# Turning eleven row blocks of a weight gradient by DMA transposes instead of TensorE transposes

## The chip, the core and the metric

One core of one Trainium2 chip runs one program: the forward pass and all gradients of a small stack of layers. The metric is the device time of one execution in microseconds. A kernel is run several times; the median is given with the lowest and highest. A profile is one execution recorded by the hardware; its span is the time from the first to the last instruction.

The engines have short names in the profile's rows: PE is TensorE (PEld its weight loads), DVE is VectorE, ACT is ScalarE, POOL is GpSimd and SP is SyncE, which here does nothing but issue DMA transfers. Each engine works through its own list of instructions in order. A "q" behind the name (SPq) marks the engine's queue of waits and DMA issues.

## The reference

Two layers are applied twice each: A, a gated long convolution (an SSM of H3 kind), and B, a dense layer with SiLU. Each has a layer norm ahead of it and a residual around it. The program returns the output and the gradients of eight inputs.

```python
def _B_ref(x, w1, w2):
    h = jnp.einsum("bsd,df->bsf", x, w1)
    h = _silu(h)
    out = jnp.einsum("bsf,fd->bsd", h, w2)
    return out

x = A_q
x = x + _A_ref(_layernorm(x, axis=-1), A_k, A_v, A_shift_k, A_ssm_k, A_ssm_D)
x = x + _B_ref(_layernorm(x, axis=-1), B_w1, B_w2)
x = x + _A_ref(_layernorm(x, axis=-1), A_k, A_v, A_shift_k, A_ssm_k, A_ssm_D)
x = x + _B_ref(_layernorm(x, axis=-1), B_w1, B_w2)
...
_out, _vjp = jax.vjp(_f, A_q, A_k, A_v, A_shift_k, A_ssm_k, A_ssm_D, B_w1, B_w2)
_grads = _vjp(grad_out)
```

The sizes are S = 2048 rows, D = 448 channels and F = 1792 hidden units, all in bf16. The gradient of `w1` has D rows and F columns. It is the sum over both uses of layer B of norm(x) transposed times the gradient of `h`.

## The kernel before

The program has three stages. `_ssm_prefix` (to about 100 us) makes the spectra of the convolution by products with Fourier matrices. `Main.run` then goes through four chunks of 512 rows, forward and backward. Last comes `_ssm_suffix` (from about 500 us), which takes the gradient of the convolution back through the spectra and makes the gradients of k, v, the shift weights, the convolution kernel and the skip weights.

The gradients of the two weights of layer B don't hang on that last stage. They are cut into small pieces by the class `Jobs`, and `jobs.run(n)` sprinkles n pieces between the suffix's own TensorE work. The order of TensorE's instructions is the order in which the program is written (`manual_schedule`). For the other engines the Tile framework's scheduler orders instructions when the program is built; on the chip each engine follows that fixed order.

One piece is four products with 128x128 stationary blocks (`mms`, L1038). The gradient of `w1` is made transposed: for each of 14 row blocks `ft` of 128 hidden units, a PSUM bank `ps_d` of 128 x 448 gathers 16 products of the stationary operand `g_d1` with the normalized rows `n3m`, then 16 of `g_d0` with `n1m` (the two uses of layer B). Each set of 16 stationary blocks is one load of 512 KB from DRAM into one of four `dstat` buffers (`load`, L1030), issued by SP as soon as TensorE is through with the load four before.

When a row block is done, `fin_w1` copies the bank to SBUF on ScalarE (`dout`, L1112, three buffers in turn) and calls `flush` for the row block before it, which thus is turned one block late. `flush` turns 128 hidden units x 448 channels into 448 channels x 128 hidden units: four TensorE transposes (L1125) of 112 columns each into the PSUM bank `ps_dt`, a ScalarE copy into one of four SBUF buffers `do7` (shown as `wts`, since they lie in that tile, L1127) and a store to the output issued by POOL (L1128). `do7` has 112 partitions, one for each of the 112 channels of a quarter.

POOL's queue also carries other stores of the suffix, among them `gkv` (L1268) and `gk` (L1254), whose SBUF buffers are reused two or four units later. ACT's queue carries the load of `kx_s` (L1275 and L1277) and the stores of `gK` (L1295). A DMA transpose is already used elsewhere: `_turn_grad` (L131, L132) turns rows of 448 channels straight from DRAM in two transfers, the first of three 128-channel blocks, the second of the last 128 channels (320 to 448, so that 64 channels come twice); `store` (L595) turns larger SBUF tiles.

Of the kernel before, what the change touches and what calls it, by code (L numbers as in the profile page):

```python
# [17 lines left out]
P = 128  # L18
# [5 lines left out]
DC = 112  # L24
ND = 4
# [88 lines left out]
def _copy(nc, eng, out, in_):  # L114
    if eng is nc.scalar:
        return nc.scalar.copy(out, in_)  # L116
    return eng.tensor_copy(out, in_)  # L117
# [18 lines left out]
def kernel(  # L136
# [63 lines left out]
    with tc.manual_schedule(engines={nc.tensor.engine}):  # L200
        with ExitStack() as es:
            Main(k, es).run(ys)
        _ssm_suffix(k)
# [790 lines left out]
class Jobs:  # L994
# [121 lines left out]
    def flush(self):  # L1116
        nc, k = self.nc, self.k
        if self.pend is None:
            return
        ft, o = self.pend  # L1120
        self.pend = None
        out7v = k.outs[7].rearrange("(c p) f -> p c f", p=DC)
        pt = k.psum.tile([DC, ND, P], BF16, name="ps_dt", tag="tr", bufs=2)
        for dc in range(ND):
            nc.tensor.transpose(pt[:, dc, :], o[:, dc * DC:(dc + 1) * DC], k.ident[:])  # L1125
        o7 = k.do7[ft % 4]
        _copy(nc, nc.vector if ft == 13 else nc.scalar, o7, pt[:])  # L1127
        (nc.scalar if ft == 13 else nc.sync if ft == 12 else nc.gpsimd).dma_start(out=out7v[:, :, ft * P:(ft + 1) * P], in_=o7)  # L1128


def _s1_gy(k, rows):
# [6 lines left out]
def _ssm_suffix(k):  # L1138
    nc, tc, bal = k.nc, k.tc, k.bal
# [7 lines left out]
    with ExitStack() as es:  # L1147
# [4 lines left out]
        gks = sp.tile([P, 19, D], BF16, name="gks")  # L1152
        ws = k.wtp.tile([P, 6144], BF16, name="wts", tag="WT")
        kk1 = ws[:, 0:4096].rearrange("p (a b) -> p a b", a=2)
        k.do7 = [ws[:DC, 4096 + 512 * i:4608 + 512 * i].rearrange("p (a b) -> p a b", a=ND) for i in range(4)]
        B1k = A1[:].rearrange("p a c n s -> p (a c n s)").rearrange("p (q d) -> p q d", d=D)
        for _ in _s1_gy(k, range(12, 16)):
            jobs.run(2)
# [18 lines left out]
        for g in range(7):  # L1177
            pt = psum.tile([P, 2, 16, 64], BF16, name="ps_tr", **mm)
# [188 lines left out]
```

## Time and profile before

| what | value |
|---|---|
| time, median of 3 runs | 704.69 us (704.58 to 705.24) |
| the profiled run's own time | 704.52 us |
| its span | 702.7 us, 14555 instructions, granted TensorE clock 0.997 |
| TensorE products ps_d, L1038, in all | 896, 353 ns listed each |
| TensorE transposes ps_dt, L1125 | 56 (14 row blocks x 4), 216 to 264 ns listed each |
| ScalarE copy of ps_dt, L116 | 13, 585 to 614 ns each |
| VectorE copy of ps_dt, L117 (row block 13) | 1, 424 ns |
| stores of w1's gradient, L1128 | 14 of 112 KB: 12 by POOL (707 to 747 ns to issue each), 1 by SP, 1 by ACT |
| loads of dstat for w1's gradient | 28 of 512 KB, median 5.4 us from issue to landing |
| queue q1 (hardware, SP's transfers) | 184550 packets, 111.78 MB, 58.3% of 16 engines' span |

The listed time of one matmul is from its start to its modelled end, and neighbours overlap in TensorE's pipeline; what one costs a full stream is the distance from its start to the next start. An instruction on a queue of SP, ACT or POOL that issues a transfer is listed with the time that issuing it took; the transfer lands later, and the rows of DMA issues give that time. A row of waits names the waiting instruction, what released it, the total in microseconds, how many times, and the longest. Times in a timeline are microseconds from the span's start. The row blocks of w1's gradient run from 580 to 695 us of the span.

### The profile page before, as it was taken

The numbers are of one execution on the slowest core, as the hardware profiler recorded it, in microseconds if no ns is written. First come the engines' busy times: TensorE is split into PE (matmuls) and PEld (weight loads), VectorE is DVE, ScalarE is ACT, GpSimd is POOL, SyncE is SP. The second block draws the span as 40 slices with busy tenths as digits, with TensorE's granted clock in tenths as the row PEclk, the third lists the DMA queues.
The fourth block names the chain that finished last, engine by engine and source line by source line (L and its number), as shares of the span: only waits on it lengthen the run. The fifth ranks groups of instructions, "written<-read, shape, count | busy, mean of one in ns | idle before, by whom it ended". The sixth has DMA issues, their size and how long they took to land.

```text
span 702.7 us, 14555 instructions
## 1 busy us (share of the span) xinstructions
PE 671.8 (96%) x5897; PEld 359.8 (51%) x5933; DVE 484.3 (69%) x1131; ACT 432.2 (62%) x522; POOL 101.0 (14%) x173
## 2 busy tenths in 40 slices
PE   6998789999999999999999999999999999999996
PEld 5876555454444444444444334444555555555664
DVE  5689862676889948889568884753946555538991
ACT  4988766968866957669577585223655453554431
POOL 1047110110011100111100100010111211102311
PEclk9999999999999999999999999999999999999999
DMA  8999948459898987487676599959567888966981
GB/s 315 260 272 304 351 137 212 112 109 260 217 225 240 245 195 184 137 236 202 203 180 180 159 227 335 288 168 218 187 225 268 309 273 317 349 190 215 330 292 42
DMA packets 199797, 161.03 MB, mean 229 GB/s; under 512 B 147697, under 2 KB 180212, under 8 KB 198962
## 3 DMA queue, kind: packets, MB, share of 16 engines
q1 hardware_dynamic: 184550, 111.78, 58.3%
q0 software_dynamic: 10368, 36.29, 15.2%
q10 hardware_dynamic: 4812, 12.04, 5.2%
q8 instruction: 46, 0.75, 0.4%
q14 instruction: 21, 0.17, 0.1%
HBM read 66.05 MB, written 54.60 MB: 172 GB/s over the span
## 4 chain that ended last, share of the span: by engine, by line
PE 59%; DVE 19%; issue 10%; ACT 5%; DMA 3%; POOL 3%; ACTq 0%; POOLq 0%; DVEq 0%
PE ps_d L1038 18%; PE ps_n L828 9%; PE ps_h L638 7%; PE ps_g L638 6%; PE ps_o L790 5%; DMA w2sb<-in_B_w_dram 3%; DVE ln_st L301 2%; PE ps_v L265 2%; PE ps_cv L449 2%; POOL rstd L306 2%; DVE lb_v L986 2%; PE ps_h L642 2%; DVE n L309 1%; DVE X L794 1%; PE ps_g L642 1%
## 5 line engine op out<-in xcount | busy, mean ns | idle before, releaser
L1038 PEld LDWEIGHTS <-dstat 128*128 128x128 bf16 x896 | 84.0, 98 | 77.8 <-issue 4.0
L828 PE MATMUL ps_n<-w1T,ghT 128*128 128x448 bf16 x448 | 97.0, 353 | 1.6 <-DVE ghT L813 1.3
L790 PE MATMUL ps_o<-w2sb,aT 128*128 128x448 bf16 x448 | 89.3, 353 | 0.2
L638 PE MATMUL ps_h<-nT,w1sb 128*128 128x512 bf16 (+1 forms) x408 | 84.2, 336 | 3.5 <-ACT Dall L116 2.2
L116 ACT CAST ghT<-ps_g 128x1024 bf16<-128x1024 f32 (+1 forms) x54 | 47.8, 900 | 59.4 <-PE ps_g L642 40.2
L638 PE MATMUL ps_g<-nT,w2T 128*128 128x512 bf16 x319 | 78.0, 380 | 2.1 <-DVE Dall L117 0.5
L828 PEld LDWEIGHTS <-ghT 128*128 128x128 bf16 x448 | 40.7, 98 | 50.5 <-issue 8.0
L790 PEld LDWEIGHTS <-aT 128*128 128x128 bf16 x448 | 43.0, 98 | 40.7 <-issue 2.6
L638 PEld LDWEIGHTS <-w1sb 128*128 128x128 bf16 x420 | 39.2, 98 | 39.0 <-issue 9.8
L773 ACT ACTIVATE aT<-ps_h 128x1024 bf16<-128x1024 f32 (+1 forms) x48 | 44.2, 920 | 20.4 <-PE ps_h L642 12.7
L986 DVE SCALAR_TENSOR_TENSOR lb_v<-lb_u,n 128x448 bf16<-128x448 bf16 x60 | 37.2, 619 | 25.4 <-ACT lb_u L832 24.9
L116 ACT CAST Dall<-ps_h 128x1024 bf16<-128x1024 f32 (+2 forms) x60 | 54.3, 906 | 0.0
L783 ACT ACTIVATE Dall<-Dall 128x1024 bf16<-128x1024 bf16 (+1 forms) x48 | 53.2, 1186 | 0.1
L638 PEld LDWEIGHTS <-w2T 128*128 128x128 bf16 x336 | 31.3, 98 | 41.9 <-issue 7.1
L306 POOL TENSOR_TENSOR rstd<-ln_ve,mhalf 128x2 f32<-128x2 f32 (+1 forms) x24 | 19.6, 818 | 220.7 <-DVE ln_ve L305 220.7
L1038 PE MATMUL ps_d<-X,dstat 128*128 128x448 bf16 x224 | 47.9, 353 | 0.0
L1038 PE MATMUL ps_d<-go,dstat 128*128 128x448 bf16 x224 | 47.2, 353 | 0.0
L1038 PE MATMUL ps_d<-n3m,dstat 128*128 128x448 bf16 x224 | 46.4, 353 | 0.0
L1038 PE MATMUL ps_d<-n1m,dstat 128*128 128x448 bf16 x224 | 46.3, 353 | 0.0
L832 ACT ACTIVATE lb_u<-ps_n,rstd 128x448 bf16<-128x448 f32 x32 | 20.6, 644 | 29.1 <-PE ps_n L828 21.2
L116 ACT CAST A1g<-ps_v 128x1024 bf16<-128x1024 f32 x14 | 14.9, 1065 | 36.5 <-PE ps_v L265 36.5
L794 DVE TENSOR_TENSOR X<-X,ps_o 128x448 bf16<-128x448 bf16 x32 | 19.5, 611 | 21.7 <-PE ps_o L790 21.7
(206 smaller groups left out, 1120.2 us busy)
## 6 DMA issues: line engine op xcount, KB each, us to landing
dstat<-a_d SPq DMA_DIRECT2D x28, 512.0 KB, 4.9
dstat<-g_d SPq DMA_DIRECT2D x28, 512.0 KB, 5.4
a_d<-turned SPq DMA_DIRECT2D x16, 512.0 KB, 3.0
g_d<-turned SPq DMA_DIRECT2D x16, 512.0 KB, 3.0
a_d<-turned SPq DMA_DIRECT2D x16, 384.0 KB, 2.7
g_d<-turned SPq DMA_DIRECT2D x16, 384.0 KB, 3.1
spec_K<-KAB POOLq DMA_DIRECT2D x7, 512.0 KB, 5.7
KAB<-KAB POOLq DMA_DIRECT2D x28, 128.0 KB, 5.0
```

What stands on the lines that cost most here:

```text
L116: return nc.scalar.copy(out, in_)
L306: nc.gpsimd.tensor_tensor(out=r[:, lo:hi], in0=ve[:, lo:hi], in1=k.mhalf[:, lo:hi], op=ALU.pow)
L638: self.nc.tensor.matmul(ps, lhsT=w[:, b, ft * P:(ft + 1) * P], rhs=x[:, b], start=(start and b == 0), stop=(stop and b == bs[2]))
L642: self.nc.tensor.matmul(ps, lhsT=w[sl, b, ft * P:(ft + 1) * P], rhs=x[sl, b], start=start, stop=stop)
L773: self.last_silu = nc.scalar.activation(aT[hh][:, o:o + hi - lo, :], ps[:, lo:hi, :], ACT.Silu)
L783: self.nc.scalar.activation(dT[hh][:, o:o + n, :], dT[hh][:, o:o + n, :], ACT.Derivative_silu)
L790: nc.tensor.matmul(po[:, :D], lhsT=aT[ft // 7][:, ft % 7, tl * P:(tl + 1) * P], rhs=self.w2sb[:, ft, :], start=(ft == 0), stop=(ft == NF - 1))
L794: self.last_o = nc.vector.tensor_tensor(out=X[:, t, :], in0=X[:, t, :], in1=po[:, :D], op=ALU.add)
L828: nc.tensor.matmul(pn[:, :D], lhsT=gh[ft // 7][:, ft % 7, tl * P:(tl + 1) * P], rhs=self.w1T[:, ft, :], start=(ft == 0), stop=(ft == NF - 1))
L832: nc.scalar.activation(u0[:], pn[:, :D], ACT.Identity, scale=k.rstd[2 * L + 1][:, t:t + 1], accum_out=cp[:, tl, 0:1])
L986: nc.vector.scalar_tensor_tensor(out=v[:], in0=u0, scalar=-1.0 / D, in1=n_t, op0=ALU.mult, op1=ALU.mult, accum_out=cp[:, 1:2])
L1038: self.nc.tensor.matmul(ps[:, :D], lhsT=st[:, t, :], rhs=mov[:, t, :], start=(first and t == 0), stop=(last and t == NT - 1))
```

## The change

For row blocks 0 to 10, `flush` no longer uses TensorE, PSUM and ScalarE. SP issues two DMA transposes from `dout` to a `do7` buffer: channels 0 to 383 as three blocks of 128, and channels 320 to 447 as a fourth, whose upper half holds the last 64 channels. POOL then stores the result in two transfers, 384 rows and 64 rows. The `do7` buffers get all 128 partitions. Row blocks 11, 12 and 13 keep the old way.

```diff
         ft, o = self.pend
         self.pend = None
+        o7 = k.do7[ft % 4]
+        fs = slice(ft * P, (ft + 1) * P)
+        if ft < 11:
+            nc.sync.dma_start_transpose(out=o7[:, 0:3, :], in_=o[:, 0:384])
+            nc.sync.dma_start_transpose(out=o7[:, 3:4, :], in_=o[:, 320:448])
+            nc.gpsimd.dma_start(out=k.outs[7][0:384, fs].rearrange("(c p) f -> p c f", p=P), in_=o7[:, 0:3, :])
+            nc.gpsimd.dma_start(out=k.outs[7][384:448, fs], in_=o7[64:128, 3, :])
+            return
         out7v = k.outs[7].rearrange("(c p) f -> p c f", p=DC)
         pt = k.psum.tile([DC, ND, P], BF16, name="ps_dt", tag="tr", bufs=2)
         for dc in range(ND):
             nc.tensor.transpose(pt[:, dc, :], o[:, dc * DC:(dc + 1) * DC], k.ident[:])
-        o7 = k.do7[ft % 4]
-        _copy(nc, nc.vector if ft == 13 else nc.scalar, o7, pt[:])
-        (nc.scalar if ft == 13 else nc.sync if ft == 12 else nc.gpsimd).dma_start(out=out7v[:, :, ft * P:(ft + 1) * P], in_=o7)
+        _copy(nc, nc.vector if ft == 13 else nc.scalar, o7[:DC], pt[:])
+        (nc.scalar if ft == 13 else nc.sync if ft == 12 else nc.gpsimd).dma_start(out=out7v[:, :, fs], in_=o7[:DC])
...
-        k.do7 = [ws[:DC, 4096 + 512 * i:4608 + 512 * i].rearrange("p (a b) -> p a b", a=ND) for i in range(4)]
+        k.do7 = [ws[:, 4096 + 512 * i:4608 + 512 * i].rearrange("p (a b) -> p a b", a=ND) for i in range(4)]
```

In the built program TensorE's order is otherwise the same. On SP each pair of transposes stands among the loads of `dstat`. On POOL the stores of w1's gradient stand at somewhat other places among those of `gkv` and `gk`, and on VectorE a few neighbouring instructions of the `gk` units (L1249, L1251, L1253, L1267) change places.

## The prediction

> **What bounds the kernel now.** I read the engine totals of the page, then the table of engine work by stretch, then TensorE's timeline inside one row block, then the waits and landings of the loads that feed it, then the rows of the transposes by DMA that the kernel already makes.
>
> ```profile
> PE 671.8 (96%) x5897; PEld 359.8 (51%) x5933; DVE 484.3 (69%) x1131; ACT 432.2 (62%) x522; POOL 101.0 (14%) x173
> ...
> core 0: us, PE busy (x) PEld busy (x) DVE busy (x) ACT busy (x) POOL busy (x), PEclk, DMA share, GB/s
> 640.00:655.00 15.00, 15.00 (x86) 7.97 (x85) 14.97 (x24) 6.40 (x10) 4.71 (x8) 1.00 0.73 236
> 655.00:670.00 15.00, 15.00 (x151) 10.67 (x150) 15.00 (x22) 6.99 (x12) 4.09 (x6) 1.00 0.99 362
> 670.00:685.00 15.00, 15.00 (x116) 8.67 (x117) 14.97 (x21) 4.99 (x9) 2.89 (x5) 1.00 0.83 280
> 685.00:697.00 12.00, 11.95 (x272) 7.57 (x272) 2.42 (x34) 1.79 (x4) 2.01 (x3) 1.00 0.15 41
> ```
>
> TensorE (PE) is busy 96% of the span and every microsecond of these stretches, at granted clock 1.00. VectorE (DVE) is as busy from 640 to 685 us, and the DMA engines are full from 655 to 670. These two are what could take the bound over.
>
> ```profile
> 624.66 2.44 PE L1038 MATMUL ps_d<-n1m,dstat 128*128 128x448 bf16 x12
> 626.94 0.39 PE L1125 MATMUL ps_dt<-ident,dout 128*112 128x128 bf16 x4
> 627.16 1.68 PE L1038 MATMUL ps_d<-n3m,dstat 128*128 128x448 bf16 x8
> ```
>
> Starts are what count here, since the listed durations overlap: twelve products in 626.94 - 624.66 = 2.28 us (0.19 each), then four transposes in 627.16 - 626.94 = 0.22 us.
>
> **What is removed.** Eleven groups of four transposes (row blocks 0 to 10, turned while the next block runs). Start to next start, in order, they took 0.22, 0.27, 0.23, 0.23, 0.22, 0.23, 0.22, 0.22, 0.22, 0.22, 0.22 us: 2.50 us of TensorE's stream. PE shows no idle time in between, so all of it comes off the end if nothing else gets late. With them go eleven copies on ScalarE (ACT, 0.59 us each, 6.5 us). ACT idles before most of its work there (dout waited 21.0 us in all for ps_d), so I count these at nothing. After the last ps_sk product the end is a chain of its own (697.6 to 702.7: DVE's gskb, ps_r, gsr, the last stores). Row blocks 11 to 13 keep the old way, and that chain is the same.
>
> The Trainium skill speaks against the change: "VectorE: DVE Perf Modes", sections "The three transpose paths" and "Rules for kernel authors", gives 390 ns for a 128x128 transpose on TensorE and 1309 ns by DMA, and advises TensorE if PSUM will do as the destination. Here the four start 0.22 us apart from what follows, some 56 ns each; by its 390 ns the eleven groups would be worth, as an estimate, 17 us instead of 2.5. The trace disagrees with that as a price in a stream.
>
> **What is added on SP.** Each row block now issues two transposes, of three and of one 128-column block. No SBUF-to-SBUF transpose of this size is in the trace. The nearest by size are L131 and L132 (same two shapes, from HBM), the nearest by source L595 (SBUF, 12 to 16 blocks):
>
> ```profile
> L131 SPq DMA_TRANSPOSE nT<-in_grad_out_dram x12: 1177/1258/1677, 182.8 to 365.9; - x12
> ...
> L132 SPq DMA_TRANSPOSE nT<-in_grad_out_dram x12: 1223/1234/1757, 184.0 to 367.2; - x12
> ...
> L595 SPq DMA_TRANSPOSE turned<-ghT x32: 1390/1625/6072, 168.8 to 489.2; - x32
> ```
>
> (minimum, median, maximum ns on the queue.) A pair costs SP between 2 x 1.2 = 2.4 and 2 x 6.1 = 12.1 us. I take 2.5: in stretches where the DMA engines were just as full (198 to 206 us, share 1.01) the long ones took 1.5 to 1.8, and none of the 24 short ones passed 1.76.
>
> What is queued behind a pair is the next 512 KB load of dstat, TensorE's stationary operand. In the built order the pair of block n stands after the load of n1m's part for block n+2 and before that of n3m's for block n+3 (the pair of block 1 one load later). The first load waits until PE is through with block n, and dout's copy comes within 1.3 us of that. The second waits for a buffer that PE frees 3 to 5 us after the first (loads were issued at 652.52, 656.53, 661.34, 666.38, 671.19, 676.23). So the pair falls into time in which SP stood waiting:
>
> ```profile
> SPq L1030 <- PE ps_d L1038: 73.2, 20, 4.7
> SPq L1030 <- PE ps_dt L1125: 26.0, 7, 4.5
> ```
>
> Only at blocks 1 and 4 does it end after the buffer is free (dout copied at 600.85 and 620.75, plus 2.5, against 602.96 and 622.96), by 0.3 to 0.4 us. That is hidden by the loads' lead: from issue to first use 11.4 to 15.6 us, to landing 3.4 to 12.3. The thinnest spare is 1.6 us (issued 592.57, landed 10.1 later, used 604.23), ahead of the first pair; then 3.3 (656.53, landed 12.3 later, used 672.11). Price: 0; at 12.1 us a pair, the rival below.
>
> **What is added on the DMA engines.** A 28-block transpose stream alone ran at 290 GB/s of full share (114.8 us on), so four blocks (128 KB) are 0.45 us of all engines, 4.9 us in all. Only the two pairs near 655 to 670 meet full engines, and may push what is in flight by 0.9 us. The cover is the spare above.
>
> **The completion counters.** In the built program the transfers of SP and ACT take eight counters in turn, and one that reuses a counter waits until its former user has landed. Two more transfers a row block make the turn shorter, and two waits begin to count. (a) n3m's load for block 12 now waits for the landing of that for block 11: issued 656.53 - 1.84, landing 12.3 later, plus up to 0.9: 667.0 to 667.9, where PE would have let it go at 666.38 - 2.06 = 664.3. It is used at 679.53 - 2.50 = 677.0, which leaves 9.1 to 10.0 us. The traffic of queue q1 falls silent near 673, about 7 us after its issue; its neighbours took 10.5 and 7.9. Spare: 3.0 to -1.4; I take 2, no stall. (b) ACT's second gK store waits for kx_s (issued 654.33, landing 13.2 later, both 1.8 earlier now: 665.7) instead of 665.91 - 2.06 = 663.9. ACT stands 1.8 us; the copies behind it (gK's dc=2) have a second PSUM buffer before PE asks, so 0.
>
> **POOL.** Eleven stores of 0.71 us become 22 of 0.55 to 0.7, 5 us more on an engine 14% busy, and they wait for a pair to land. A pair is issued when dout is copied, 4 to 10 us before the old transposes ran, so its store is ready no later than before. In the full stretch gk and gkv stores stand behind block 8's. VectorE's gk two units later reuses a buffer that the third gk store (658.98, landing 9.0 later) freed 1.0 us ahead of need, so VectorE may lose 0.5 to 2 us. It is 0.97 us ahead of ps_sk at 686.05, and the third ps_sk group needs its bank only at 691.9: 5.4 us of cover. Price 0.
>
> **Sum.** 702.7 - 2.5 = 700.2 us of span. The profiled run took 704.52, 1.8 around its span, and the median is 704.69, so 704.69 - 2.5 = 702.2 us.
>
> **Rivals.**
> 1. *Given back where the DMA engines are full.* n3m's load for block 12, or the one after, lands 1 to 2.5 us late through (a) and the added traffic, and PE waits. For: share 0.99, landings of 12.3. Against: no PE wait on a load today, and 2 us of spare. Some 704.0, from 703.3 to 704.7.
> 2. *Slower: SP is held by the pairs.* If a transpose behind a full ring holds SP 4 to 6 us, as L595's did at 159.0 (4.03) and 438.9 (6.07), block 8's pair (issued 653.05 - 1.84 = 651.2) ends at up to 663.3, and n3m's load for block 11 lands at 663.3 + 12.3 = 675.6 against use at 672.11 - 2.28 = 669.8: 5.8 us of stall, 1.7 at 4 us a transpose. It makes the kernel slower once the pair takes over 669.8 + 2.5 - 12.3 - 651.2 = 8.8 us: about 707, up to 708. Against: the short ones never did so.
> 3. *VectorE's gk chain becomes the bound.* POOL's new order holds gk stores by more than 5.4 us: PE waits for ps_sk's bank; 704 to 705.5. For: DVE has no gaps from 640 to 685.
> 4. *Each transpose held PE for all its listed 0.22 us:* 44 x 0.22 = 9.7 us, 695.0. The starts speak against it. The 390 ns of the Trainium skill's "VectorE: DVE Perf Modes", section "The three transpose paths", points this way.
>
> **How the numbers follow.** Forecast 0.60 (own range 701.6 to 703.2), rival 1 0.17, rival 2 0.15, rival 3 0.06, rival 4 0.02. A measurement here can tell 0.2% from nothing, 1.4 us: faster is under 703.3, slower over 706.1. Faster: 0.60 + 0.02 + a sliver of rivals 1 and 3, 0.63. Same: most of 1 and 3, 0.21. Slower: 0.16. The range runs from 701.4 (2.5 plus the 0.7 by which runs differ) to 706.0, which takes in forecast and rivals 1 and 3.
>
> **What would show it.** Right: starts of ps_d follow one another at 0.19 us where ps_dt stood; PE without gaps to the last ps_sk, 2.5 us earlier; pairs near 2.5 us on SP; loads still waiting for PE. Wrong: idle time of PE before L1038 released by a dstat load between 655 and 680, L1125's pairs above 4 us, or ps_sk waiting for skjunk.

## The result and the profile after

| | median of the runs | lowest to highest | ratio to before |
|---|---|---|---|
| before | 704.38 us (6 runs) | 703.32 to 705.24 | |
| after | 713.91 us (6 runs) | 708.59 to 717.54 | 1.0124 [1.0096, 1.0152] |
| forecast | 702.2 us | 701.4 to 706.0 | |

The change costs 9.5 us where 2.5 were to be gained, and its runs lie 9 us apart where those of before lie within 2. The profiled execution took 716.18 us with a span of 714.2 (before: 704.52 and 702.7). A ratio leaves out runs more than 1.5% above the fastest of their kernel and isn't the quotient of the medians, which are over all runs, so where a kernel scatters the two differ a little.

First the page of after: the engine totals, the queue of SP's transfers, the products ps_d with n3m (at the right the idle time ahead of them and who ended it), and the loads of `dstat` for w1's gradient with their median from issue to landing.

```profile
PE 672.1 (94%) x5853; PEld 357.1 (50%) x5889; DVE 484.2 (68%) x1131; ACT 427.3 (60%) x511; POOL 108.4 (15%) x184
...
q1 hardware_dynamic: 190886, 113.22, 59.5%
...
L1038 PE MATMUL ps_d<-n3m,dstat 128*128 128x448 bf16 x224 | 46.5, 353 | 4.1 <-DMA dstat<-g_d 4.1
...
dstat<-g_d SPq DMA_DIRECT2D x28, 512.0 KB, 7.8
```

PE has 44 instructions less, as many as the eleven groups had, and is no less busy in microseconds. The loads land 7.8 us after their issue instead of 5.4, and PE now waits for them. Queue q1 moved only 1.3% more bytes and was busy for 1.2 points more of the span: by the totals hardly anything was added.

The engine work by stretch in after (from before, the four stretches from 640 us on were shown; there 610 to 625 us had PE at 15.00, a DMA share of 0.84 and 293 GB/s).

```profile
core 0: us, PE busy (x) PEld busy (x) DVE busy (x) ACT busy (x) POOL busy (x), PEclk, DMA share, GB/s
610.00:625.00 15.00, 12.51 (x182) 6.74 (x180) 3.40 (x6) 5.02 (x6) 2.35 (x4) 1.00 1.13 267
625.00:640.00 15.00, 12.52 (x172) 6.60 (x171) 4.98 (x8) 5.50 (x6) 3.47 (x5) 0.89 0.75 177
640.00:655.00 15.00, 15.00 (x81) 7.67 (x80) 13.65 (x22) 5.50 (x7) 4.84 (x9) 1.00 0.80 223
655.00:670.00 15.00, 15.00 (x125) 9.48 (x123) 15.00 (x23) 6.01 (x8) 5.83 (x9) 1.00 0.98 323
670.00:685.00 15.00, 14.74 (x127) 9.25 (x125) 7.07 (x11) 6.54 (x11) 3.72 (x7) 1.00 1.06 284
685.00:697.00 12.00, 10.26 (x173) 5.80 (x174) 10.71 (x15) 1.33 (x3) 2.75 (x6) 1.00 0.83 224
```

From 610 to 625 us the DMA share rose from 0.84 to 1.13 while the rate fell from 293 to 267 GB/s. (Share and rate count the packets that begin in a stretch, each with its whole time and all its bytes, so a share can pass 1.) Engines that count as busy and move less are the first sign of what happened: packets were open for longer. PE lost time in two places, 610 to 640 and after 670, and between them none.

PE's timeline in after at these places (start, length, instruction, and in brackets the idle time ahead with its releaser).

```profile
618.22 0.93 PE L1038 MATMUL ps_d<-n1m,dstat 128*128 128x448 bf16 x4
621.64 3.20 PE L1038 MATMUL ps_d<-n3m,dstat 128*128 128x448 bf16 x16 [2.49 <-DMA dstat<-g_d]
...
628.41 0.20 PE L265 MATMUL ps_v<-Gsb,pab 64*128 64x64 bf16 x2 [2.08 <-DVE pab L1211]
...
629.56 4.06 PE L1038 MATMUL ps_d<-n1m,dstat 128*128 128x448 bf16 x12
633.41 1.79 PE L1038 MATMUL ps_d<-n3m,dstat 128*128 128x448 bf16 x8
...
683.81 0.93 PE L1038 MATMUL ps_d<-n1m,dstat 128*128 128x448 bf16 x4
686.31 3.20 PE L1038 MATMUL ps_d<-n3m,dstat 128*128 128x448 bf16 x16 [1.56 <-DMA dstat<-g_d]
689.94 2.44 PE L1038 MATMUL ps_d<-n1m,dstat 128*128 128x448 bf16 x12 [0.44 <-DMA dstat<-g_d]
...
701.37 1.47 PE L1321 MATMUL ps_sk<-kx_s,gks 128*32 128x128 bf16 x64 [1.99 <-DVE skjunk L1324]
702.77 3.68 PE L1038 MATMUL ps_d<-n1m,dstat 128*128 128x448 bf16 x12
706.38 1.07 PE L1321 MATMUL ps_sk<-kx_s,gks 128*32 128x128 bf16 x32
```

Five waits are new: three for a `dstat` load, one for VectorE's pab (2.08 us, with 0.40 more on its next part) and one for skjunk. The last of the forecast's signs of error is there too, ps_sk waiting for skjunk. After some of the waits PE is also slower for a while: the twelve products at 629.56 take 633.41 - 629.56 = 3.85 us in place of 2.28, in a stretch with a granted clock of 0.89. In single microseconds (columns as in the table above, the clock third from the right) that mean comes apart:

```profile
622.00:623.00 1.00, 1.00 (x7) 0.52 (x6) 0.00 (x0) 0.00 (x0) 0.00 (x0) 1.00 0.97 366
...
631.00:632.00 1.00, 1.00 (x5) 0.39 (x3) 0.36 (x1) 0.00 (x0) 0.75 (x1) 0.50 0.85 311
...
687.00:688.00 1.00, 1.00 (x7) 0.49 (x5) 1.00 (x3) 0.00 (x0) 0.00 (x0) 1.00 0.78 170
...
703.00:704.00 1.00, 1.00 (x4) 0.44 (x3) 0.60 (x9) 0.00 (x0) 0.00 (x0) 0.50 0.58 128
```

The granted clock is halved twice, for 3.4 us each, from 630.2 and from 701.9 us, after the waits for pab and for skjunk. After the two long waits for `dstat`, at 621.64 and 686.31, it stays at 1.00.

Two of VectorE's own waits in after, from 580 us on (what was waited for: us in total, times, longest), say why it was late.

```profile
DVE wts L1243 <- DMA wts<-in_A_shift_k_dram: 11.3, 1, 11.3
...
DVE gk L1260 <- DMA out_dram<-gk: 9.2, 2, 7.9
```

The first, for the load of the shift weights, was 3.9 us before (that load now lands 12.3 us after its issue instead of 4.9). The second, for gk's stores to leave their buffers, is not in the list of before. Both are waits for late transfers, so the new waits of PE lead back to the DMA engines.

### The profile page after: what moved, and what is told of

Read it like the earlier page. It is cut to its first block, busy times and chain, and to the rows that moved or that the text cites. A ratio compares the mean times of both kernels' runs of the same rounds, so it can differ in the third digit from the quotient of the medians.

```text
span 714.2 us, 14522 instructions
## 1 busy us (share of the span) xinstructions
PE 672.1 (94%) x5853; PEld 357.1 (50%) x5889; DVE 484.2 (68%) x1131; ACT 427.3 (60%) x511; POOL 108.4 (15%) x184
## 4 chain that ended last, share of the span: by engine, by line
PE 62%; DVE 15%; issue 8%; DMA 7%; ACT 5%; POOL 2%; POOLq 0%; ACTq 0%; DVEq 0%
PE ps_d L1038 21%; PE ps_n L828 9%; PE ps_h L638 7%; PE ps_g L638 5%; PE ps_o L790 5%; DMA w2sb<-in_B_w_dram 3%; DVE ln_st L301 2%; PE ps_cv L449 2%; PE ps_v L265 2%; DMA dstat<-g_d 2%; POOL rstd L306 2%; DMA wts<-dout 2%; DVE lb_v L986 2%; PE ps_h L642 2%; DVE n L309 1%
## 5 line engine op out<-in xcount | busy, mean ns | idle before, releaser
L1038 PE MATMUL ps_d<-n1m,dstat 128*128 128x448 bf16 x224 | 49.1, 368 | 0.4 <-DMA dstat<-g_d 0.4
```

The source lines that it names most:

```text
L1038: self.nc.tensor.matmul(ps[:, :D], lhsT=st[:, t, :], rhs=mov[:, t, :], start=(first and t == 0), stop=(last and t == NT - 1))
```

## The experiments

Two theories were set against each other. M: the DMA engines stop while a transpose is under way and one of its parts is missing, so a pair costs other transfers far more than its bytes. W: the extra transfers as such do it, by their places in the queues, their completion counters or POOL's two stores; S is its form in which the small packets do it.

### Plain copies in the place of the transposes

```diff
-            nc.sync.dma_start_transpose(out=o7[:, 0:3, :], in_=o[:, 0:384])
-            nc.sync.dma_start_transpose(out=o7[:, 3:4, :], in_=o[:, 320:448])
+            nc.sync.dma_start(out=o7[:, 0:3:2, :], in_=o[:, 0:256].rearrange("p (c f) -> p c f", f=P))
+            nc.sync.dma_start(out=o7[:, 1:4:2, :], in_=o[:, 192:448].rearrange("p (c f) -> p c f", f=P))
```

> The two transposes of a row block become two plain copies of 64 KB each from dout to do7, cut so that each makes 256 packets of 256 B: the same bytes and the same 512 packets as a pair of transposes, in the same places of every queue, with the same waits and stores. Rows 0 to 1407 of the transposed gradient come out unturned. Theory M (the DMA engines stop while a transpose is under way and its slowest part is missing): no stops, no wait of TensorE on a dstat load, the 2.5 us that the prediction counted come off: about 702, and runs as close together as those of before. Rival W (the added transfers, queue places, completion counters and stores make the loads late, whatever the transfers do) and rival S (it is the many 256 B packets): as slow as the change, 709 to 717.

Measured: 702.46 us (701.63 to 703.47) against 704.21, ratio 0.9977 [0.9967, 0.9987]. With every engine's order, the counters and the stores as in the changed kernel, and the same 128 KB in packets of 256 bytes, the loss is gone. W and S fall. What is left over is the gain that was forecast, 1.75 us of it by the medians. One thing besides the turning differs: a copy held SP for 0.61 us and a transpose for 1.23 to 1.39, by the medians. That isn't the cause of PE's first wait, since the load that it waited for was issued at 607.81 us with the change and at 607.79 with the copies, and landed 13.8 and 8.2 us later.

Since PE's order is the same in both kernels, the loss can be laid out instruction by instruction. The same stretches of PE's timeline with the plain copies, and ahead of them the one wait for a load that is left there:

```profile
603.90 1.69 PE L1038 MATMUL ps_d<-n3m,dstat 128*128 128x448 bf16 x8 [0.48 <-DMA dstat<-g_d]
...
618.21 0.93 PE L1038 MATMUL ps_d<-n1m,dstat 128*128 128x448 bf16 x4
618.97 3.19 PE L1038 MATMUL ps_d<-n3m,dstat 128*128 128x448 bf16 x16
...
626.17 1.68 PE L1038 MATMUL ps_d<-n3m,dstat 128*128 128x448 bf16 x8
...
676.46 0.93 PE L1038 MATMUL ps_d<-n1m,dstat 128*128 128x448 bf16 x4
677.23 3.19 PE L1038 MATMUL ps_d<-n3m,dstat 128*128 128x448 bf16 x16
680.25 2.43 PE L1038 MATMUL ps_d<-n1m,dstat 128*128 128x448 bf16 x12
...
690.62 2.44 PE L1038 MATMUL ps_d<-n1m,dstat 128*128 128x448 bf16 x12
692.99 1.07 PE L1321 MATMUL ps_sk<-kx_s,gks 128*32 128x128 bf16 x32
```

How far the changed kernel is behind at the same instruction:

| instruction | changed - copies | behind, us |
|---|---|---|
| n1m x4 | 618.22 - 618.21 | 0.01 |
| n3m x16, first wait | 621.64 - 618.97 | 2.67 |
| n3m x8, after pab and the slower clock | 633.41 - 626.17 | 7.24 |
| n1m x4 | 683.81 - 676.46 | 7.35 |
| n3m x16, second wait | 686.31 - 677.23 | 9.08 |
| n1m x12 | 689.94 - 680.25 | 9.69 |
| n1m x12, after skjunk | 702.77 - 690.62 | 12.15 |
| ps_sk x32 | 706.38 - 692.99 | 13.39 |

The changed kernel is not behind up to 618 us, although four pairs have been issued by then and two stops, listed below, have passed, and it loses next to nothing from 633 to 683. The waits make up 2.49 + 2.08 + 0.40 + 1.56 + 0.44 + 1.99 = 8.96 us, and the other 4.4 us is PE running slower around them: two stretches of 3.4 us at half the clock are 3.4 us of it (the two groups of twelve at 629.56 and 702.77 alone are 1.57 and 1.24 us longer than with the copies). In these two executions the spans differ by 714.2 - 700.6 = 13.6 us, so the table holds nearly all of it.

What the DMA engines did is in the trace's packet records. Kilobytes begun in each half microsecond, worked out from them:

```
from us      610.0  610.5  611.0  611.5  612.0  612.5  613.0  613.5  614.0  614.5
changed        173    148      7     15     36     15     22     72     26    232
copies         208    201    205    219    209    199    188    175    183    205
```

From 611.0 to 614.5 us hardly anything begins but single packets of 256 bytes (transposes) and of 7168 bytes (`ksf`, the suffix's 1.8 MB load on ACT's queue), while 16 packets or more are open together; eighteen of the 7168-byte ones, usually 0.27 us, took 1.6 to 3.8. Fifteen of these began between 610.58 and 610.61 and stood open until 612.2 to 614.4. Beside them the next packets of 256 and of 7168 bytes, with start in us and bytes, follow one another like the work of one engine:

```
changed: 610.96 256, 610.98 7168, 611.25 256, 611.27 7168, 611.53 256, 611.55 7168, 611.82 256, 611.83 7168, 612.10 256, 612.11 7168
```

One part of a transpose, then one packet of `ksf`, then the next part. The records don't name the engine, so it is a reading, not shown, that one engine still had parts of the transpose to do and the other fifteen waited for it. A stop of this kind is counted here as time in which at least eight packets are open together, each of under 8 KB and open for over 0.9 us in all. From 594 to 705 us it comes to 16.6 us with the change and 0.9 before; with the copies there is none:

```
changed: stops (start + length, us) 606.8+1.5 610.6+4.0 623.3+1.4 628.6+1.4 646.2+0.9 676.6+4.1 687.0+2.8 690.2+0.5
```

The two long ones come ahead of PE's early and late loss. `ksf` landed 16.7 us after its issue in place of 10.1 with the copies.

### Three pairs where the queues are quiet, three where they are not

```diff
-        if ft < 11:
+        if ft in (5, 6, 7):
```

> Only row blocks 5, 6 and 7 are turned by DMA; their pairs fall between 627 and 648 us, where the DMA engines are half idle (share 0.52 to 0.73 in the kernel before) and ACT's queue has hardly any load in flight. Theory M: stops need other traffic, so each pair costs at most a short one; gain 0.22 + 0.22 + 0.22 = 0.67 us: 703.7 to 704.4. If each pair stops the engines as long whatever else is in flight, loads are still hidden here by 8 us of spare: the same. Rival W: a third of the loss or less, up to 707.

Measured: 703.88 us (703.18 to 705.66), ratio 0.9998 [0.9989, 1.0007]. No stop in its profile, and no wait of PE for a load.

```diff
-        if ft < 11:
+        if ft in (2, 3, 4):
```

> Only row blocks 2, 3 and 4 are turned by DMA; their pairs fall between 603 and 625 us, beside the load of ksf (1.8 MB) and of the shift weights on ACT's queue. Theory M: the three pairs stop the engines for some 1.5, 3.8 and 1.5 us, ksf lands at 14 us or more instead of 9, n3m's load for block 5 later than 11 us after its issue, and TensorE waits: about half of the loss, 706 to 711, with waits on dstat near 621 us. Rival W: counters and queue places of three row blocks cost little, under 705.

Measured: 704.46 us (703.07 to 708.11), ratio 1.001 [0.9997, 1.0022]. The loss that was expected isn't there. Its profile does have stops, 5.1 us in all (607.5+1.2, 617.2+2.3, 623.7+1.6), and yet PE waits for no load. So a stop is not yet a loss: the loads have spare, and a few stops use it up without showing.

### One transpose of four blocks in the place of three and one

```diff
-        return self.k.dp2.tile([P, D], BF16, name="dout", tag="dout", bufs=3)
+        return self.k.dp2.tile([P, 512], BF16, name="dout", tag="dout", bufs=3)
...
+        self.nc.gpsimd.memset(o[:, D:], 0.0)
...
-            nc.sync.dma_start_transpose(out=o7[:, 0:3, :], in_=o[:, 0:384])
-            nc.sync.dma_start_transpose(out=o7[:, 3:4, :], in_=o[:, 320:448])
+            nc.sync.dma_start_transpose(out=o7[:, 0:4, :], in_=o[:, 0:512])
```

> dout is widened to 512 columns (the last 64 set to 0 by POOL, 14 small extra instructions), so that one transpose of four blocks does what the pair did; everything is computed. Theory M in the form that a stop comes once for each transpose: half of the stops, about half of the 12 us of loss (9.5 measured and 2.5 of gain) goes: 706 to 709. In the form that the stop comes with the bytes or once a row block: 709 to 717 as the change. Rival W: one transfer and one counter less a row block, somewhat better than the change, 706 to 712; this run alone does not decide between M and W, e1_copy does.

Measured: 723.49 us (719.53 to 727.2), ratio 1.0273 [1.0237, 1.0308]: worse than the change, whose interval ends at 1.0152. PE's waits in it, from 580 us on:

```profile
PE ps_d L1038 <- DMA dstat<-g_d: 9.4, 4, 5.5
PE ps_sk L1321 <- DVE skjunk L1324: 6.8, 1, 6.8
```

They are the same two kinds as in the changed kernel, but longer, and the stops come to 22.3 us. That a pair costs one stop for each of its transfers finds no support here. The run isn't a clean comparison, though: POOL's small memsets stand among its stores, which wait for transposes to land, and SP stood 4.2 us for them, up to 1.8 at a time. Whether one transfer of four blocks by itself stops the engines for longer than two of three and one stays open.

### The large load moved ahead, with all eleven pairs and with eight

In the first of these kernels the load of `ksf` is issued three steps of the suffix earlier, before the pairs begin; the second also leaves blocks 8, 9 and 10 to TensorE. A third is the kernel before with the load moved, as a control.

```diff
+            if cp == 2:
+                ksf = sp.tile([P, 2, J, D // 2], BF16, name="ksf")
+                with tc.issue_after(k.last_x.ins):
+                    nc.scalar.dma_start(out=ksf[:], in_=k.KS_d[:].rearrange("h p j d -> p h j d"))
...
-                ksf = sp.tile([P, 2, J, D // 2], BF16, name="ksf")
-                with tc.issue_after(k.last_x.ins):
-                    nc.scalar.dma_start(out=ksf[:], in_=k.KS_d[:].rearrange("h p j d -> p h j d"))
```

> The change with the 1.8 MB load of ksf (ACT's queue) issued some 40 us earlier, ahead of the first transposes; nothing else moves. Theory M: the transposes of blocks 1 to 4 no longer meet packets of another hardware queue there; the stop of 3.8 us at 610.6 and the wait of TensorE at 621 go, together with their echo (wait on VectorE and lower clock): some 5 to 7 of the 12 us, so 705 to 709. If other traffic on SP's own queue and POOL's suffices for the stops: no better than the change, 709 to 717.

> As the run with ksf earlier, and transposes by DMA in row blocks 0 to 7 alone, none beside the loads of kx_s and the stores of gK after 655 us. Theory M: most of the foreign traffic is away; of 8 x 0.23 = 1.84 us of gain most remains if TensorE waits on no load: 702.5 to 704. If stops beside the dstat loads alone are enough: 705 to 710.

> The kernel before with the load of ksf issued some 40 us earlier: the control for the two runs above. Every theory: no wait of TensorE on this load before, so no change, 703.8 to 704.8.

Measured:

| kernel | median, us | lowest to highest | ratio to before |
|---|---|---|---|
| load ahead, all eleven | 713.46 | 707.4 to 717.31 | 1.0122 [1.0063, 1.0182] |
| load ahead, blocks 0 to 7 | 702.65 | 701.71 to 703.68 | 0.9974 [0.9965, 0.9984] |
| load ahead, no pairs | 704.54 | 703.13 to 706.43 | 1.0 [0.999, 1.001] |

With all eleven the time is no better than that of the change, a miss. PE's timeline of that kernel shows that the early loss is gone and the late one is not:

```profile
671.66 1.05 PE L1300 MATMUL ps_gK<-Minvs,A1g 128*112 128x128 bf16 x16 [1.83 <-ACT gK L1301]
...
684.33 3.20 PE L1038 MATMUL ps_d<-n3m,dstat 128*128 128x448 bf16 x16 [2.45 <-DMA dstat<-g_d]
...
698.46 1.08 PE L1322 MATMUL ps_sk<-kx_s,gks 128*32 128x128 bf16 x64 [1.66 <-DVE skjunk L1325]
```

These are the only new waits; from 594 us to the first of them PE has no idle time. Its span is 709.7 us against 700.6 with eight pairs, so here the late loss alone is some 9 us, where the changed kernel lost 6 after 683 us. The work by stretch of the same kernel, with all eleven pairs, where the late loss begins:

```profile
655.00:670.00 15.00, 14.83 (x147) 10.38 (x145) 13.61 (x19) 4.77 (x7) 1.46 (x2) 1.00 1.02 204
670.00:685.00 15.00, 10.76 (x69) 5.95 (x69) 3.17 (x5) 5.64 (x9) 4.82 (x8) 0.89 1.09 302
```

And with pairs for blocks 0 to 7 only:

```profile
655.00:670.00 15.00, 15.00 (x158) 10.81 (x156) 15.00 (x22) 8.01 (x12) 3.42 (x6) 1.00 1.01 399
670.00:685.00 15.00, 15.00 (x159) 8.68 (x157) 14.22 (x26) 4.02 (x8) 3.33 (x6) 1.00 0.69 223
```

At the same DMA share, 1.02 and 1.01, one moves 204 GB/s and the other 399. The share says that packets are open, not that anything moves. The six microseconds in which it happens, with eleven pairs and with eight:

```profile
657.00:663.00 6.00, 6.00 (x63) 4.30 (x61) 6.00 (x10) 2.98 (x5) 0.00 (x0) 1.00 0.07 27
...
657.00:663.00 6.00, 6.00 (x69) 4.42 (x67) 6.00 (x9) 3.32 (x6) 1.08 (x2) 1.00 0.97 402
```

In the first, beside the pair of block 8, fifteen packets of 14336 bytes (`kx_s`) stand open for 6.1 to 7.2 us in place of 0.54 and end by 663.1, while for the first four of these six microseconds single parts of the transpose and single packets of 14336 bytes take turns, as at 611 us in the changed kernel. This is the longest stop in any of these traces, and the count above, made for packets of under 8 KB, doesn't see it; the sums of stops are lower bounds. The two `dstat` loads issued at 655.42 and 660.23 landed 17.4 and 17.1 us later. The kernel with eight pairs keeps 1.87 us of the gain, beats both the kernel before and the changed one, and its control says that the moved load alone is worth nothing. Eight pairs without the moved load were not tried.

### The first five, and the last three

```diff
-        if ft < 11:
+        if ft < 5:
```

> Transposes by DMA in row blocks 0 to 4 alone. Blocks 2 to 4 alone cost nothing that could be measured, since three stops fit into the loads' spare. Theory M with spare used up in a row: five pairs in 30 us push the loads past the spare; the wait near 621 us comes back: 706 to 711. If the loss of the change were made after 655 us alone: 703.1 (gain 5 x 0.24 = 1.2).

Measured: 708.73 us (704.9 to 717.05), ratio 1.0041 [1.0025, 1.0058]. Its one wait for a load, from PE's timeline:

```profile
623.64 5.39 PE L1038 MATMUL ps_d<-n3m,dstat 128*128 128x448 bf16 x16 [4.69 <-DMA dstat<-g_d]
```

Its packet records have a stop of 4.9 us at 610.4, and PE's mean clock is 0.88 from 610 to 625 us and 0.90 from there to 640. Blocks 0 to 4 thus bring the early loss alone, where blocks 2 to 4 brought none.

```diff
-        if ft < 11:
+        if ft in (8, 9, 10):
```

> Transposes by DMA in row blocks 8, 9 and 10 alone, beside the load of kx_s and the stores of gK (655 to 680 us). With ksf earlier, eight pairs cost nothing and eleven cost 9 us, so these three should hold nearly all of that. Theory M: three pairs stop engines that are full (share 0.99 in the kernel before); waits of TensorE on dstat near 680 us: 706 to 713. If the loss needs all eleven pairs (something that adds up over the row blocks): 704.0 (gain 0.66).

Measured: 707.0 us (705.29 to 716.16), ratio 1.0038 [1.0009, 1.0067]. The last three cost something, 2.5 us by the medians, but far from the 10.8 us that leaving them out saved (713.46 - 702.65). Its profile, of a run of 705.29 us, has stops of 6.2 us and no stop at 657 us. What eight earlier pairs add to the late loss was not tried by itself.

### The pairs alone

The kernel before, with TensorE's transposes as they were, and the eleven pairs besides, into a buffer that nobody reads and nobody stores (two halves in turn, where the change has four buffers).

```diff
+        if ft < 11:
+            d7 = k.dd7[ft % 4]
+            nc.sync.dma_start_transpose(out=d7[:, 0:3, :], in_=o[:, 0:384])
+            nc.sync.dma_start_transpose(out=d7[:, 3:4, :], in_=o[:, 320:448])
...
+        dd7 = sp.tile([P, 2, 512], BF16, name="dd7")
+        k.dd7 = [dd7[:, i % 2].rearrange("p (a b) -> p a b", a=ND) for i in range(4)]
```

> The kernel before, TensorE's transposes and POOL's stores as they were, plus the eleven pairs of DMA transposes in the places that they have in the change, into a buffer that nobody reads. Theory M: the whole cost without the gain of 1.8 to 2.5 us: 711 to 720. If the cost came from the stores that wait for the pairs, or from what VectorE and POOL do in another order: about 704.5.

Measured: 712.31 us (706.21 to 717.11), ratio 1.0088 [1.0058, 1.0117]. Without POOL's split stores, without a reader and with nothing taken from PE, the pairs alone cost 7.8 us by the medians. Together with the plain copies this fixes the cause on the transposing itself, from both sides: added alone it costs, and taken out alone it leaves the gain.

### The large load in four parts

The kernel with the first five pairs, and `ksf` in four transfers with packets of 1792 bytes in place of 7168.

```diff
-                    nc.scalar.dma_start(out=ksf[:], in_=k.KS_d[:].rearrange("h p j d -> p h j d"))
+                    for q in range(4):
+                        nc.scalar.dma_start(out=ksf[:, :, 4 * q:4 * q + 4, :], in_=k.KS_d[:, :, 4 * q:4 * q + 4, :].rearrange("h p j d -> p h j d"))
```

> Blocks 0 to 4 by DMA (708.7 us), with the load of ksf cut into four transfers, so that its packets are 1792 B instead of 7168 B; the same bytes on the same queue at the same time. Theory M with the detail that the slowest engine takes a packet of the other queue between two parts of the transpose: the stop at 610 us shrinks from 3.8 to some 1 us, and the time to 703.5 to 706. If the stop depends on the bytes of the other load alone: 706 to 712 as without the cut.

Measured: 710.38 us (705.5 to 715.81), ratio 1.008 [1.0051, 1.0108], no better than 708.73 with the load in one piece; a miss. The long stop at 610 us is gone (4.4 us in all in place of 10.5), and so is PE's wait for `dstat`. But the load of the shift weights landed 11.0 us after its issue, and VectorE made PE wait:

```profile
627.43 0.20 PE L265 MATMUL ps_v<-Gsb,pab 64*128 64x64 bf16 x2 [3.58 <-DVE pab L1211]
```

The size of the neighbour's packets bears on how long one stop is, as far as one execution tells; that fits the turns taken at 611 us. The time of this kernel didn't get better by it.

### Two more quiet pairs

The kernel with the load ahead and eight pairs, and blocks 11 and 12 by DMA as well. Their pairs were issued at 681.1 and 688.5 us, where the DMA share of before was 0.53 (681 to 685 us) and 0.15 (from 685).

```diff
-        if ft < 8:
+        if ft < 8 or ft in (11, 12):
```

> ksf earlier, and blocks 0 to 7, 11 and 12 by DMA (8, 9, 10 and 13 by TensorE): the pairs of 11 and 12 fall after 675 us, when kx_s has landed. Theory M: the gain of ten groups, 10 x 0.23 = 2.3 us, against 1.9 of the run with eight: 702.0 to 702.6. If the last two meet the last dstat loads and gK's stores: 702.6 to 704.5.

Measured: 703.57 us (701.81 to 705.82), ratio 0.9978 [0.9959, 0.9998]. No better than eight pairs at 702.65: 2 x 0.22 us more was to be gained, and the sum of stops in its profile is 7.7 us against 5.5.

## Why the prediction was wrong, point by point

**What is removed: right.** With eight pairs and no wait of PE for a load, 1.87 us are gained by the medians, where the first eight of the eleven groups had been found to take 1.84. With the plain copies in all eleven places it is 1.75 us (0.9 to 2.3 by the interval of the ratio), where 2.50 were worked out; in the profiled run 0.48 of the rest is the wait at 603.90, for the load whose spare of 1.6 us the prediction had called the thinnest. In the changed kernel itself the seam is clean: PE starts sixteen products at 607.61 and the next eight at 610.64, 3.03 us for 16 x 0.19, where the transposes used to stand between.

**What is added on SP: right.** The rows of the two transposes on SP's queue in after (minimum, median and maximum ns; first and last start):

```profile
L1125 SPq DMA_TRANSPOSE wts<-dout x11: 1196/1234/1577, 596.3 to 680.3; - x11
```

The second, of one block, has a median of 1386 ns and a maximum of 2539. The medians add up to 2.6 us against 2.5, and no pair can have held SP for more than 1.58 + 2.54 = 4.1 us, under half of the 8.8 at which rival 2 would have begun to make the kernel slower. That rival had the sign of the result and not its mechanism.

**What is added on the DMA engines: this step failed.** It priced a pair at 128 KB by 290 GB/s, 0.45 us of all engines, 4.9 us in all, and covered that by the spare of the loads. The rate came from a stream of transposes that had the engines to itself, and in that stream the packets took 18 ns each with no stop. Beside `dstat`, `ksf` and POOL's stores the eleven pairs made the engines stop for 16.6 us in eight stops of 0.5 to 4.1 us. A pair's landing shows it as well: the transpose of three blocks took 4.0 to 14.7 us from issue to landing, with a median of 7.9. The loads issued around it landed up to 13.9 us after their issue, and the 1.6 and 3.3 us of spare, which were counted against one pair at a time, had to serve for several in a row. That blocks 2 to 4 cost nothing measurable, blocks 0 to 4 some 4 us and blocks 5 to 7 nothing shows that the price isn't so much per pair.

The bounds were the failing of method here. The two ends for a pair's cost to the other transfers should have come from the nearest rows *beside traffic*, and the trace of before had them: the large turn at L595 held its queue for 6.07 us at 438.9 at worst, against a median of 1.6. It was read as a risk to SP alone. The DMA engines in before at that place, from 438 to 448 us in 40 slices:

```profile
DMA  9999999999999999999999960002999999999994
GB/s 481 373 387 401 409 416 416 387 430 416 401 444 401 402 416 430 394 394 356 366 274 203 71 39 22 29 16 51 284 289 289 291 294 243 283 283 268 261 268 125
```

From 443.5 to 445 us the rate falls to between 16 and 71 GB/s while that turn is under way, and its packets of 256 bytes stand open for 1.1 to 1.9 us. By the count above the kernel before has fourteen such stops ahead of 594 us, of 0.5 to 1.9 us, every one with a DMA transpose in flight. So the missing term was there to be read before the change was made.

**The completion counters and POOL: right as terms, and used up by the stops.** With the plain copies the counters and the queues are the same, and VectorE already waits 4.6 us for gk's stores, more than the 0.5 to 2 that were forecast, inside the cover of 5.4. With the transposes this wait is 9.2 us, the cover is gone, and PE waits 1.99 us for skjunk. Rival 3 named the place; POOL's order is not the cause. The counters also pass a late landing on as a late issue. On SP one pair of the changed kernel stood 3.5 us for the late landing of `ksf`, whose counter it takes over. And (a) came true: n3m's load for block 12 was issued at 675.23 us, right behind the landing of that for block 11 at 675.16 (with the copies 665.22, behind 665.15).

**Rival 1** had the second wait for `dstat` right, in its place and its path: the load for which PE waited 1.56 us at 686.31 is n3m's for block 12, held up through (a), and with the 0.44 us at 689.94 it comes to about the 1.8 us that was priced. But of the 11.0 us that this load took to land (7.2 with the copies) 4.1 fall on the stop at 676.6, in which little moves, where the rival counted bytes that are added; and the early loss, at a DMA share of 0.84, lay outside of it.

**The Trainium skill.** Its advice in "VectorE: DVE Perf Modes", section "Rules for kernel authors", to use TensorE if PSUM will do as the destination, was the right one for the late blocks. Its price of 390 ns was not the reason: eleven groups were worth 1.75 us, some 40 ns a transpose. In "Advanced Engine Details and Errata", section "X-Bar Transpose (TRN2)", the Trainium skill says that transposes by DMA are as fast as regular ones on this chip. The plain copies and the transposes, equal in bytes and place, differ here by 702.46 against 713.91 us.

**What stays open:** why only some pairs bring a long stop, how far the reading that one engine is waited for holds beyond the two stops at which it was followed, whether one transfer of four blocks is by itself worse than three and one, and how much of the late loss is owed to the pairs before block 8.

## What to carry to other kernels

Price a DMA transpose by what it does to the transfers beside it, and not by its bytes: put a plain copy of the same bytes in its place, and the difference is that price. The spare of the loads is one account for all transposes whose stops fall within it, so a few can be free where more of them are not; here eight of fourteen blocks, with the large load moved out of their way, gave 0.9974 [0.9965, 0.9984], and eleven gave a loss. Look for stretches with a falling rate beside the transposes that a kernel already makes. A DMA share near 1 means open packets; read it beside the rate.

## What was not expected of the hardware

- Beside a DMA transpose fifteen packets stood open on the 16 DMA engines for 6 us (at 657 us with the load ahead), and as little as 7 KB began in half a microsecond (at 611 us in the changed kernel) where 205 began with plain copies.
- At a DMA share of 1.02 and 1.01 the same stretch moved 204 and 399 GB/s.
- After two of the changed kernel's five waits (2.08 with 0.40 us, and 1.99 us) PE's granted clock was halved for 3.4 us, and twelve products took 3.85 us in place of 2.28; after one of 2.49 us it stayed full. All in all the waits cost about half as much again (13.39 us behind for 8.96 us of waits).
